# Filler products for TensorE in layer 1 and gate weights in three loads, in a two-layer decode kernel

## The chip, the cores and the metric

The kernel runs on one core of one Trainium2 chip. The metric is the device time of one execution in microseconds (us). Executions of one kernel agree here within about 0.3%, so a change of a few tenths of a microsecond is at the edge of what the times can show.

## The reference, cut to what matters

One token goes through two layers with the same weights. Each layer is an attention over the last 4096 positions of a cache (32 heads of width 192), then a gated feed-forward part (640 to 1536 to 640). Both add to a residual.

```python
x = x + A(layernorm(x), k_cache, v_cache, wq, wo)   # softmax(q k^T) v, 32 heads, window 4096
x = x + B(layernorm(x), w_gate, w_up, w_down)       # down(sigmoid(gate(x)) * up(x))
x = x + A(layernorm(x), ...)                        # the same weights and cache again
x = x + B(layernorm(x), ...)
```

With one token there is almost no reuse. The kernel keeps a part of the cache on the chip for the second layer, but it still reads 218 MB in 0.51 ms.

## The kernel before

Heads go in 16 pairs. The keys of pair p and the values of pair p-1 come in one load of 7.3 MB (128 rows of 56,832 B, 7,104 KB in the views), into alternating buffers. All big loads are issued in order on one queue; each waits until TensorE has finished with the buffer it will overwrite. A step of layer 1 (`l == 0` in the code), cut:

```python
def step(p, prev):
    if l == 0 and prev > 0:
        ev = PVn(prev - 1, 1 - prev % 2)   # output projection of an older pair; frees its value buffer
    Q(p, 0)                                # query, waits for the load of pair p
    QK(p, 0)                               # scores, 24 products of 512 columns
    soft(0, ...)                           # DVE maximum, ACT diag, PE transpose of it, DVE
    expo()                                 # ACT exponential
    PVmm(prev, prev % 2)                   # value products, 32 of 384 columns
    ET(p % 2)
    PVt(prev % 2)
```

After the steps comes the last pair, whose values are in three pieces, and then the feed-forward part. Its weights pass through one region that holds 19 blocks of 640 columns, so the later loads overwrite blocks whose products are done (cut, with `...`):

```python
# key: (cell of the region, first block, end block)
MW = {"wg0": (0, 0, 3), "wg1": (3, 3, 6), "wg2": (6, 6, 9), "wg3": (9, 9, 12), "u0": (12, 0, 2), "u1": (14, 2, 7),
      "d0": (0, 0, 3), "d1": (3, 3, 6), "u2": (6, 7, 10), "u3": (9, 10, 12), "d2": (11, 6, 9), "d3": (14, 9, 11), "d4": (16, 11, 12)}
MD = {"wg0": (0, 0, 6), "wg2": (6, 6, 12), ...}      # the loads: gate weights in two, the rest as in MW
MAFTER = {"d0": ("wg0",), "d1": ("wg1",), "u2": ("wg2",), "u3": ("wg3",), ...}   # d0 is loaded after the products of wg0
...
            PVmm(p, 1)          # end of layer 1, p = 15
            RS(1, 2)
            PVn(p - 1, 0)
            PVt(1, False)
            PVn(p, 1)
        return residual(xi)     # then layer norm, gate, up and down products
```

## Time and profile before

| what | value |
|---|---|
| median of 6 runs (lowest to highest) | 513.63 us (513.21 to 513.99) |
| read from HBM | 218.2 MB, 426 GB/s over the span |
| TensorE busy | 51% of the span, mean granted clock 0.623 |
| chain of waits | 64% DMA, 22% TensorE |

The page of the kernel before: busy times, then the span in 40 slices (granted clock and DMA share in tenths, and GB/s), the chain that ended last, and the group of value products (busy us and mean ns of one, then idle time before them).

```profile
PE 262.5 (51%) x3716; PEld 138.4 (27%) x3716; DVE 101.5 (20%) x385; ACT 85.1 (17%) x171; POOL 4.3 (1%) x31
...
PEclk9955665565566775566575578675655566555855
DMA  9999999999999999999999999999999999999996
GB/s 426 426 427 426 427 430 428 430 453 444 426 430 430 431 435 426 430 448 444 399 420 412 409 440 434 432 430 427 450 439 435 430 430 439 431 431 413 434 424 280
...
DMA 64%; PE 22%; DVE 8%; ACT 3%; issue 2%; SPq 1%; DVEq 0%; POOL 0%; ACTq 0%; POOLq 0%
...
L494 PE MATMUL o<-big,et_sb 128*2 128x384 bf16 x1024 | 77.4, 471 | 8.5 <-DMA big<-in_uc_dram 4.2
```

The DMA row is at its highest step in 39 of 40 slices, and the chain is mostly DMA. The table of windows for the same kernel, with the stretch where layer 1 ends:

```profile
core 0: us, PE busy (x) PEld busy (x) DVE busy (x) ACT busy (x) POOL busy (x), PEclk, DMA share, GB/s
40.00:240.00 200.00, 93.24 (x1233) 45.72 (x1233) 35.77 (x125) 30.24 (x60) 1.07 (x12) 0.60 1.00 432
257.70:288.00 30.30, 18.20 (x342) 12.17 (x338) 5.24 (x29) 4.35 (x10) 0.09 (x1) 0.58 1.00 411
277.00:288.00 11.00, 6.38 (x154) 5.63 (x154) 1.22 (x8) 0.73 (x3) 0.00 (x0) 0.50 1.02 398
```

The last three columns are the ones to read: clock, DMA share, GB/s. (These views count a packet, with its bytes and its time, where it starts. In a window of a few us rates and shares are therefore rough.) In the steps the stream moves 432 GB/s. Around the feed-forward part it moves 411, in its core 398 (share 1.02).

The timeline of TensorE in the kernel before (start, duration, then in brackets the idle time before and what ended it):

```profile
246.85 0.56 PE L414 MATMUL bank<-sh,big 128*128 128x1 bf16 x15 [5.94 <-DMA big<-in_uc_dram]
...
252.27 0.80 PE L448 MATMUL bank<-diag,sc 128*128 128x128 f32 x2 [1.76 <-ACT diag L445]
253.00 2.73 PE L494 MATMUL o<-big,et_sb 128*2 128x384 bf16 x32
...
274.86 0.96 PE L684 MATMUL scores<-sh,big 128*128 128x1 bf16 x30 [0.61 <-DVE bank L670]
277.15 0.96 PE L684 MATMUL scores<-sh,big 128*128 128x1 bf16 x30 [1.34 <-DMA big<-in_wg_dram]
...
279.85 0.83 PE L684 MATMUL scores<-sh,big 128*128 128x1 bf16 x25 [1.05 <-DMA big<-in_wu_dram]
```

The first lines are one step: TensorE waits 5.94 us for the pair load, later 1.76 us for diag, then takes 2.73 us for the value products at half clock. The last three are the gate and up products.

### The profile page before, as it was taken

The numbers are of one execution on the slowest core, as the hardware profiler recorded it, in microseconds if no ns is written. First come the engines' busy times: TensorE is split into PE (matmuls) and PEld (weight loads), VectorE is DVE, ScalarE is ACT, GpSimd is POOL, SyncE is SP. The second block draws the span as 40 slices with busy tenths as digits, with TensorE's granted clock in tenths as the row PEclk, the third lists the DMA queues.
The fourth block names the chain that finished last, engine by engine and source line by source line (L and its number), as shares of the span: only waits on it lengthen the run. The fifth ranks groups of instructions, "written<-read, shape, count | busy, mean of one in ns | idle before, by whom it ended". The sixth has DMA issues, their size and how long they took to land.

```text
span 512.2 us, 8583 instructions
## 1 busy us (share of the span) xinstructions
PE 262.5 (51%) x3716; PEld 138.4 (27%) x3716; DVE 101.5 (20%) x385; ACT 85.1 (17%) x171; POOL 4.3 (1%) x31
## 2 busy tenths in 40 slices
PE   0352455344643254436566767774725344634565
PEld 0221222122311122222234424442312122312234
DVE  0221212112210221112121343231202112210311
ACT  1110111011100111011121024221211011101220
POOL 0010000000000000000000000000000000000000
PEclk9955665565566775566575578675655566555855
DMA  9999999999999999999999999999999999999996
GB/s 426 426 427 426 427 430 428 430 453 444 426 430 430 431 435 426 430 448 444 399 420 412 409 440 434 432 430 427 450 439 435 430 430 439 431 431 413 434 424 280
DMA packets 9676, 218.47 MB, mean 427 GB/s; under 512 B 1208, under 2 KB 1592, under 8 KB 4664
## 3 DMA queue, kind: packets, MB, share of 16 engines
q1 hardware_dynamic: 9512, 218.14, 99.2%
q8 instruction: 13, 0.21, 0.1%
q10 hardware_dynamic: 144, 0.06, 0.0%
q14 instruction: 7, 0.06, 0.0%
HBM read 218.20 MB, written 0.00 MB: 426 GB/s over the span
## 4 chain that ended last, share of the span: by engine, by line
DMA 64%; PE 22%; DVE 8%; ACT 3%; issue 2%; SPq 1%; DVEq 0%; POOL 0%; ACTq 0%; POOLq 0%
DMA big<-in_uc_dram 54%; PE scores L432 8%; DMA big<-in_wd_dram 6%; PE o L494 6%; DMA big<-in_wu_dram 4%; DVE sc L442 3%; PE bank L448 2%; ACT e_sb L458 2%; PE bank L414 2%; PE bank L529 1%; SPq L217 1%; PE bank L464 1%; ACT diag L445 1%; DVE sc L477 1%; DVE qs L420 1%
## 5 line engine op out<-in xcount | busy, mean ns | idle before, releaser
L432 PE MATMUL scores<-big,qs 128*32 128x512 bf16 x744 | 82.0, 608 | 10.3 <-DVE qs L420 9.6
L414 PE MATMUL bank<-sh,big 128*128 128x1 bf16 x465 | 17.0, 166 | 130.9 <-DMA big<-in_uc_dram 128.5
L494 PE MATMUL o<-big,et_sb 128*2 128x384 bf16 x1024 | 77.4, 471 | 8.5 <-DMA big<-in_uc_dram 4.2
L445 ACT ACTIVATE diag<-cst,sc 128x128 f32<-128x128 bf16 x32 | 12.8, 401 | 304.8 <-DVE sc L442 296.8
L442 DVE TENSOR_REDUCE sc<-scores 128x1 f32<-128x1024 f32 x31 | 37.9, 1224 | 77.8 <-PE scores L432 77.8
L414 PEld LDWEIGHTS bank<-sh,big 128*128 128x128 bf16 x465 | 14.6, 103 | 134.0 <-DMA big<-in_uc_dram 112.2
L448 PE MATMUL bank<-diag,sc 128*128 128x128 f32 x64 | 22.5, 447 | 46.7 <-ACT diag L445 46.7
L458 ACT ACTIVATE e_sb<-scores,sc 128x1024 bf16<-128x1024 f32 x31 | 37.4, 1205 | 42.1 <-DVE sc L453 39.9
L494 PEld LDWEIGHTS o<-big,et_sb 128*2 128x2 bf16 x1024 | 28.4, 107 | 44.2 <-issue 29.9
L420 DVE TENSOR_TENSOR qs<-bank,cst 128x96 bf16<-128x96 f32 x30 | 7.7, 258 | 159.6 <-PE bank L414 159.6
L432 PEld LDWEIGHTS scores<-big,qs 128*32 128x32 bf16 x744 | 24.3, 131 | 43.0 <-issue 29.5
L448 PEld LDWEIGHTS bank<-diag,sc 128*128 128x128 f32 x64 | 14.1, 276 | 72.7 <-ACT diag L445 70.4
L501 ACT CAST o_sb<-o 128x384 bf16<-128x384 f32 x64 | 29.7, 474 | 22.7 <-PE o L494 22.4
L529 PE MATMUL bank<-sh,big 128*128 128x1 bf16 x480 | 17.1, 165 | 14.9 <-DVE sh L518 14.9
L468 DVE CAST et_sb<-bank 128x64 bf16<-128x64 f32 x32 | 7.2, 225 | 71.1 <-PE bank L464 71.1
L529 PEld LDWEIGHTS bank<-sh,big 128*128 128x128 bf16 x480 | 14.5, 99 | 17.4 <-DVE sh L518 12.1
L449 DVE TENSOR_REDUCE sc<-bank 128x2 f32<-128x128 f32 x32 | 9.3, 292 | 43.3 <-PE bank L448 43.3
L464 PE MATMUL bank<-cst,e_sb 128*128 128x8 bf16 x256 | 11.7, 169 | 6.8 <-ACT e_sb L458 6.7
L464 PEld LDWEIGHTS bank<-cst,e_sb 128*128 128x128 bf16 x256 | 9.0, 102 | 23.0 <-issue 16.5
L475 PE MATMUL o<-sc 128*128 128x2 f32 x62 | 13.7, 291 | 0.6 <-ACT o_sb L501 0.6
L475 PEld LDWEIGHTS o<-sc 128*128 128x128 f32 x62 | 11.8, 239 | 2.0 <-ACT o_sb L501 1.3
L477 DVE RECIPROCAL sc<-o 64x1 f32<-64x1 f32 x62 | 10.2, 165 | 9.5 <-PE o L475 7.9
(80 smaller groups left out, 109.5 us busy)
## 6 DMA issues: line engine op xcount, KB each, us to landing
big<-in_uc_dram SPq DMA_DIRECT2D x20, 7104.0 KB, 22.6
big<-in_uc_dram SPq DMA_DIRECT2D x11, 3552.0 KB, 20.6
big<-in_uc_dram SPq DMA_DIRECT2D x2, 3072.0 KB, 18.6
big<-in_uc_dram SPq DMA_DIRECT2D x8, 480.0 KB, 7.4
big<-in_uc_dram SPq DMA_DIRECT2D x1, 2784.0 KB, 13.3
big<-in_uc_dram SPq DMA_DIRECT2D x1, 2304.0 KB, 10.7
big<-in_uc_dram SPq DMA_DIRECT2D x1, 2048.0 KB, 12.1
big<-in_wg_dram SPq DMA_DIRECT2D x2, 960.0 KB, 16.2
```

What stands on the lines that cost most here:

```text
L414: ins = t.matmul(qe[:, i:i + 1], lhsT=w[:, c * 2 * DH + c0:c * 2 * DH + c0 + P], rhs=xq[:, c:c + 1], start=(c == 0), stop=(c == DC - 1))
L432: ins = t.matmul(sc_x[1 + b][32 * j:32 * j + 32, :], lhsT=qs[:, y, k, :], rhs=slot(sa, WQE + k * W + (4 * b + j) * 512, 512), start=(k == ...
L442: pg.op("dve", lambda v: v.reduce_max(out=mx, in_=sc_x[0][:], axis=AX.X), wr=[res("mx")], ex=sc_x[3:5])
L445: pg.op("act", lambda a: a.mul(out=diag[:], in_=ident, mul=mx), rd=[res("cst"), res("mx")], wr=[res("diag")])
L448: pg.op("pe", lambda t: t.matmul(dmx[:, 0:P], lhsT=ones_f, rhs=diag[:], start=True, stop=True), rd=[res("diag"), res("ones")], ex=[rb[2]])
L458: pg.op("act", lambda a: a.activation(out=e_sb[:], in_=sc_x[0][:], func=ACT.Exp, bias=nbias, scale=srs_c, accum_out=rowsum), rd=[res("nbia ...
L464: ins = t.matmul(qe[:, 0:2 * NB].rearrange("p (r x) -> p r x", r=2)[:, :, 4 * b:4 * b + 4], lhsT=e_sb[:, b * P:(b + 1) * P], rhs=sel, star ...
L475: pg.op("pe", lambda t: t.matmul(sm, lhsT=ones_f, rhs=rs2[z], start=True, stop=True), rd=[res(f"rs2{z}"), res("ones")], wr=[res("rsum")], ...
L477: rb[bk].last["dve"] = pg.op("dve", lambda v, h=h: v.reciprocal(out=Rn[z][64 * h:64 * h + 64], in_=sm[64 * h:64 * h + 64, h:h + 1]), rd=[r ...
L494: ins = t.matmul(o8[h][32 * j:32 * j + 2, 0:2 * DH].rearrange("p (a d) -> p a d", a=2), lhsT=et_sb[:, z, h * NB + 2 * u:h * NB + 2 * u + 2 ...
L501: pg.op("act", lambda a, h=h: a.copy(out=o8_sb[:, :, h * DH:(h + 1) * DH], in_=o8[h][:, 0:2 * DH].rearrange("p (a d) -> p a d", a=2)), wr= ...
L529: ins = t.matmul(yT[:, j:j + 1], lhsT=wo[:, c * D + j * P:c * D + (j + 1) * P], rhs=oTb[z][:, c:c + 1], start=False, stop=(c == 2), skip_g ...
```

## The change

The intent: if TensorE is kept busier, its granted clock should rise. So products that nobody uses are put into its waits, into PSUM banks (the buffers that its results go to in this kernel) that are idle then. Faster value products should release buffers earlier. And the gate weights come as 3, 6 and 3 blocks in place of 6 and 6, so that the first products, and the loads that wait for them, start earlier.

```diff
-    MD = {"wg0": (0, 0, 6), "wg2": (6, 6, 12), ...}
+    MD = {"wg0": (0, 0, 3), "wg1": (3, 3, 9), "wg3": (9, 9, 12), ...}
+        def spin(n, *bks):
+            for i in range(n):
+                bk = bks[i % len(bks)]
+                m = 2 * DH if bk in (4, 5) else 512
+                pg.op("pe", lambda t, bk=bk, m=m: t.matmul(bank[bk][:, 0:m], lhsT=ident, rhs=slot(...), start=True, stop=True), ...)
-        def PVmm(p, z):
+        def PVmm(p, z, mid=None):
+                    if part == 0 and mid is not None:
+                        mid()                      # ahead of the last piece of the last values
             Q(p, 0)
             QK(p, 0)
+            if l == 0:
+                spin(3, 4, 5)
             soft(0, ...)
-            PVmm(p, 1)
+            spin(4, 0, 1)
+            PVmm(p, 1, lambda: spin(2, 0, 1))
```

More of the change, by code (lines that the diff above doesn't have):

```diff
@@ L186, in decode_kernel @@
           "d0": (0, 0, 3), "d1": (3, 3, 6), "u2": (6, 7, 10), "u3": (9, 10, 12), "d2": (11, 6, 9), "d3": (14, 9, 11), "d4": (16, 11, 12)}
-    MD = {"wg0": (0, 0, 6), "wg2": (6, 6, 12), **{k: v for k, v in MW.items() if k[0] != "w"}}
+    MD = {"wg0": (0, 0, 3), "wg1": (3, 3, 9), "wg3": (9, 9, 12), **{k: v for k, v in MW.items() if k[0] != "w"}}
     MAFTER = {"d0": ("wg0",), "d1": ("wg1",), "u2": ("wg2",), "u3": ("wg3",), "d2": ("wg3", "u0"), "d3": ("u1",), "d4": ("u1",)}
@@ L438, in QK @@
             return ev
+        def spin(n, *bks):
+            for i in range(n):
+                bk = bks[i % len(bks)]
+                m = 2 * DH if bk in (4, 5) else 512
+                pg.op("pe", lambda t, bk=bk, m=m: t.matmul(bank[bk][:, 0:m], lhsT=ident, rhs=slot(A_SLOT[0][0], WQE, m), start=True, stop=True),
+                      rd=[res("cst"), rslot[A_SLOT[0][0]]], ex=[rb[bk]])
         def soft(x=0, hook=None, mid=None, late=None):
```

## The prediction

> **What bounds the kernel now.** The DMA stream. The page puts the DMA share in the highest step in 39 of 40 slices, with 218.2 MB read at 426 GB/s over a span of 512.2 us; the chain of work that ended last is 64% DMA, 22% PE; TensorE is busy 51%. In the table of windows, 40 to 240 us has DMA share 1.00 and 432 GB/s; the stretch that the change aims at, 257.7 to 288 us, also has 1.00, but 411 GB/s. From the trace's packet records I count about 16 packets in flight in every microsecond from 2 to 506 us, so an earlier release has no hole to fill. The lower rate goes with packet size: packets of 56,832 B took 2,099 ns (433 GB/s over 16 engines), of 7,680 B 292 ns (420), of 3,840 B 154 ns (400).
>
> **What the change does.**
> 1. Wide products (three of 384 columns) go between scores and softmax in the 15 steps of the first layer, six of 512 around its last value product. Nothing uses them. They fall into waits that the timeline shows: TensorE idle from 250.5 to 252.3 us (reduction 1.24 us, diag 0.41), 266.9 to 268.5 and 269.6 to 270.3. I estimate 0.32 us for 384 columns at clock 0.50 from the score products (0.43 us between groups of 512); three are about 1 us, inside the 1.8 us wait. Their purpose is a warm clock: the Trainium skill, "TensorE: Matmul & The Clock Gate", section "Part 1: The HAM clock gate (the 'warmup' mystery)", says that some 3.4 us of sustained activity lifts the clock from half. Scores plus filler are 3.8 us, so some value products should shorten from 2.7 us (32 matmuls) towards 1.6. This trace agrees that the clock matters: scores took 2.75 us at 0.50, 1.84 where it was near full.
> 2. Releases then come perhaps 0.5 to 1 us earlier. But a pair load is issued 10.8 us after the last landing, while the one in flight takes 16.6 us (7.1 MB at 433 GB/s): 6 us of slack. The burst issued from 257.7 us is queued 5 to 19 us ahead of landing. Worth nothing in time.
> 3. Gate weights as 3, 6, 3 blocks: the first products wait for the layer norm (274.86 us, released by DVE) anyway; the middle six start about 1.1 us earlier than 277.15, the last three land as before. Up and down weights still bound the rest (each group waits for DMA). Cost: 128 packets of 7,680 B become 256 of 3,840 B: 128 x (2 x 154 - 292) / 16 = 0.13 us on a saturated stream, and one more issue of 0.43 us on a queue far ahead.
>
> **Share on the critical path.** Fillers none; of the split, the 0.13 us.
>
> **Predicted time:** 513.8 us, 8 in 10 between 513.0 and 514.6. Chances: faster by over 2% 0.01, within 2% 0.98, slower by over 2% 0.01.
>
> **What would show it.** Right: mean clock above 0.62, busy time of value products (77.4 us) down by 5 to 20 us, waits for pair loads up by as much, DMA share and GB/s of the slices kept, and 33.4 us per two pair landings kept. Wrong: GB/s of 257 to 290 us above 420, or pair landings coming earlier.
>
> **What would make it wrong.** Fillers ending so late that releases overrun the 6 us of slack; the longer loop body fetching instructions again during the loop (16 KB packets of 0.9 us each); a shifted fetch hitting the last loads, at most 0.9 us; the chip's scatter of a few tenths.

## More of the kernel before

The view of the issuing queue has the first two loads of down weights; they wait for the first gate products:

```profile
275.45 0.80 SPq L217 DMA_DIRECT2D big<-in_wd_dram  x2
```

## The result, and the profile after

| kernel | median of 6 runs (lowest to highest) |
|---|---|
| before | 513.63 us (513.21 to 513.99) |
| after | 513.72 us (513.59 to 514.20) |

The ratio is 1.0003, with a 95% interval of 0.999 to 1.0016: no difference is resolved. (Here and below a ratio is the mean time of one kernel's runs over that of the other's of the same rounds, so not quite the ratio of the medians.)

The page of the changed kernel, with the lines that answer to those of before. Line numbers moved: L494 is L503 now, and L444 is the filler.

```profile
PE 265.9 (52%) x3766; PEld 137.2 (27%) x3767; DVE 101.7 (20%) x385; ACT 84.2 (16%) x171; POOL 4.2 (1%) x31
...
PEclk9996777677756655557686588765857555556655
DMA  9999999999999999999999999999999999999996
GB/s 417 439 423 426 423 432 427 435 444 435 444 426 435 427 435 426 430 444 448 398 422 415 410 436 441 429 427 430 453 448 430 430 426 430 427 436 419 432 424 280
...
DMA 68%; PE 19%; DVE 7%; ACT 2%; issue 2%; SPq 1%; DVEq 0%; POOL 0%; ACTq 0%; POOLq 0%
...
L503 PE MATMUL o<-big,et_sb 128*2 128x384 bf16 x1024 | 68.1, 426 | 8.1 <-DMA big<-in_uc_dram 3.3
...
L444 PE MATMUL o<-big,cst 128*128 128x384 bf16 x45 | 15.4, 474 | 0.0
```

The clock row is higher in most slices of layer 1, and the value products fell from 77.4 to 68.1 us. The 45 fillers of the steps cost 15.4 us of busy time. DMA share is the same in every slice, and so is the mean of GB/s. The table of windows:

```profile
40.00:240.00 200.00, 99.25 (x1272) 47.23 (x1272) 36.20 (x126) 29.83 (x60) 1.06 (x12) 0.64 1.00 432
257.70:288.00 30.30, 20.40 (x338) 12.29 (x339) 5.08 (x28) 4.14 (x10) 0.09 (x1) 0.68 1.00 413
277.00:288.00 11.00, 6.00 (x140) 5.25 (x139) 1.13 (x7) 0.73 (x3) 0.00 (x0) 0.50 1.02 406
```

The steps (40 to 240 us) kept 432 GB/s at a clock of 0.64 in place of 0.60. The timeline of TensorE after the change, two steps and the end of the layer:

```profile
217.33 1.14 PE L444 MATMUL o<-big,cst 128*128 128x384 bf16 x3
...
219.90 2.73 PE L503 MATMUL o<-big,et_sb 128*2 128x384 bf16 x32
...
250.85 0.85 PE L444 MATMUL o<-big,cst 128*128 128x384 bf16 x3
...
253.10 1.47 PE L503 MATMUL o<-big,et_sb 128*2 128x384 bf16 x32
...
271.41 0.65 PE L503 MATMUL o<-big,et_sb 128*2 128x384 bf16 x8
...
275.13 0.54 PE L696 MATMUL scores<-sh,big 128*128 128x1 bf16 x15 [0.35 <-DVE sc L374]
276.06 0.96 PE L696 MATMUL scores<-sh,big 128*128 128x1 bf16 x30 [0.39 <-DMA big<-in_wg_dram]
277.22 0.56 PE L696 MATMUL scores<-sh,big 128*128 128x1 bf16 x15 [0.20 <-DMA big<-in_wg_dram]
```

Both steps have the three fillers. After the one at 217.33 the value products are still cold (2.73 us), after the one at 250.85 they are warm (1.47). Of 15 steps, 10 had warm value products in this trace and 3 in that of before. The last piece of the last values started at 271.41 us, against 270.28 before: at this place the fillers delayed TensorE.

The clock records kept with the traces say when the clock was granted. In the kernel before it was full for 3.4 or 6.8 us in 12 of the 15 steps as well, but in nine of these too late for the value products: in the step around 50 us these ran from 52.0 to 54.7 us at a clock of 0.50, and the clock was full from 54.5 to 57.9. After the change it was full from 49.9 to 56.7 us, and the value products took 1.47 us from 52.1 on. In each of the fourteen traces all changes of the clock lie on one grid of 3.41 us. Five such intervals are 17.1 us and a step is 16.7 us, so the grid shifts by 0.3 us from step to step. That fits warm steps coming in runs of several.

The first loads of down weights, which the split was to bring forward, were issued 0.25 us later than before (275.45):

```profile
275.70 1.28 SPq L217 DMA_DIRECT2D big<-in_wd_dram  x2
```

The time that the faster products saved became waiting. The list of waits, kernel before and then after (us in total, times, longest):

```profile
PE bank L414 <- DMA big<-in_uc_dram: 128.5, 21, 11.8
```

```profile
PE bank L414 <- DMA big<-in_uc_dram: 136.5, 22, 12.0
```

Waiting for the pair loads rose by 8.0 us, about the 9.3 us by which value products became shorter. In the kernel before the next pair load was issued about 10 us after the landing before it in a step with warm value products, and about 11 us after it in a cold one; so it was after the change. The change made more steps warm, and the pairs still landed every 16.7 us.

### The profile page after: what moved, and what is told of

It is laid out like the page before. It is cut to its first block, busy times and chain, and to the rows that moved or that the text cites. A ratio compares the mean times of both kernels' runs of the same rounds, so it can differ in the third digit from the quotient of the medians.

```text
span 512.2 us, 8685 instructions
## 1 busy us (share of the span) xinstructions
PE 265.9 (52%) x3766; PEld 137.2 (27%) x3767; DVE 101.7 (20%) x385; ACT 84.2 (16%) x171; POOL 4.2 (1%) x31
## 4 chain that ended last, share of the span: by engine, by line
DMA 68%; PE 19%; DVE 7%; ACT 2%; issue 2%; SPq 1%; DVEq 0%; POOL 0%; ACTq 0%; POOLq 0%
DMA big<-in_uc_dram 58%; PE scores L432 7%; DMA big<-in_wd_dram 6%; PE o L503 5%; DMA big<-in_wu_dram 4%; DVE sc L449 3%; PE bank L455 2%; PE bank L414 2%; PE bank L538 1%; ACT e_sb L465 1%; SPq L217 1%; ACT diag L452 1%; PE bank L471 1%; DVE sc L484 1%; DVE qs L420 1%
## 5 line engine op out<-in xcount | busy, mean ns | idle before, releaser
L414 PE MATMUL bank<-sh,big 128*128 128x1 bf16 x465 | 17.1, 166 | 138.4 <-DMA big<-in_uc_dram 136.5
L503 PE MATMUL o<-big,et_sb 128*2 128x384 bf16 x1024 | 68.1, 426 | 8.1 <-DMA big<-in_uc_dram 3.3
L503 PEld LDWEIGHTS o<-big,et_sb 128*2 128x2 bf16 x1024 | 26.2, 100 | 39.1 <-issue 20.5
L455 PE MATMUL bank<-diag,sc 128*128 128x128 f32 x64 | 19.9, 403 | 32.3 <-ACT diag L452 32.3
L455 PEld LDWEIGHTS bank<-diag,sc 128*128 128x128 f32 x64 | 12.4, 241 | 53.2 <-ACT diag L452 51.6
L471 PE MATMUL bank<-cst,e_sb 128*128 128x8 bf16 x256 | 11.6, 169 | 11.1 <-ACT e_sb L465 11.0
L444 PE MATMUL o<-big,cst 128*128 128x384 bf16 x45 | 15.4, 474 | 0.0
L484 DVE RECIPROCAL sc<-o 64x1 f32<-64x1 f32 x62 | 10.2, 165 | 9.0 <-PE o L482 7.5
(84 smaller groups left out, 124.0 us busy)
## 6 DMA issues: line engine op xcount, KB each, us to landing
big<-in_uc_dram SPq DMA_DIRECT2D x1, 2048.0 KB, 11.4
```

What stands on the lines that cost most here:

```text
L414: ins = t.matmul(qe[:, i:i + 1], lhsT=w[:, c * 2 * DH + c0:c * 2 * DH + c0 + P], rhs=xq[:, c:c + 1], start=(c == 0), stop=(c == DC - 1))
L444: pg.op("pe", lambda t, bk=bk, m=m: t.matmul(bank[bk][:, 0:m], lhsT=ident, rhs=slot(A_SLOT[0][0], WQE, m), start=True, stop=True), rd=[res ...
L455: pg.op("pe", lambda t: t.matmul(dmx[:, 0:P], lhsT=ones_f, rhs=diag[:], start=True, stop=True), rd=[res("diag"), res("ones")], ex=[rb[2]])
L471: ins = t.matmul(qe[:, 0:2 * NB].rearrange("p (r x) -> p r x", r=2)[:, :, 4 * b:4 * b + 4], lhsT=e_sb[:, b * P:(b + 1) * P], rhs=sel, star ...
L484: rb[bk].last["dve"] = pg.op("dve", lambda v, h=h: v.reciprocal(out=Rn[z][64 * h:64 * h + 64], in_=sm[64 * h:64 * h + 64, h:h + 1]), rd=[r ...
L503: ins = t.matmul(o8[h][32 * j:32 * j + 2, 0:2 * DH].rearrange("p (a d) -> p a d", a=2), lhsT=et_sb[:, z, h * NB + 2 * u:h * NB + 2 * u + 2 ...
```

## The experiments

Four theories were tried against each other:

- **A**: the DMA stream is the bound and has reserve; TensorE's time does not matter until about 6 us of slack per step are used up.
- **B**: the chain through TensorE bounds, and the fillers' own time eats what they save.
- **C**: the fillers gain and the finer gate loads lose as much.
- **D**: the end of layer 1, where the end fillers and the new split act, is bound by TensorE.

### The two halves of the change alone

Fillers only, gate weights as before:

```diff
-    MD = {"wg0": (0, 0, 3), "wg1": (3, 3, 9), "wg3": (9, 9, 12), ...}
+    MD = {"wg0": (0, 0, 6), "wg2": (6, 6, 12), ...}
```

> Only the fillers, gate weights in two loads of six as before. Theory A (the DMA stream is the bound, TensorE has about 6 us of slack per step): same as before, 513.6 within 0.3 us. Rival C (fillers gain, the split of the gate weights costs as much, and the two cancel): faster than before by 0.3 us or more. Rival B (the chain through TensorE bounds, and the fillers' 17 us of busy time eat the 9 us that they save): no clear difference either; B is told apart by the runs with more fillers.

Measured: 513.58 us (5 runs), ratio 0.9997 (0.9983 to 1.001).

The split only, no fillers:

```diff
-    MD = {"wg0": (0, 0, 6), "wg2": (6, 6, 12), ...}        # in the kernel before
+    MD = {"wg0": (0, 0, 3), "wg1": (3, 3, 9), "wg3": (9, 9, 12), ...}
```

> Only the gate weights in 3, 6, 3 blocks, no fillers. Theory A: before plus about 0.1 us (estimate from packet times of before: 128 x (2 x 154 - 292) / 16 = 0.13 us), so 513.6 to 513.9, not resolved. Rival C: slower than before by 0.3 us or more.

Measured: 513.55 us (5 runs), ratio 0.9996 (0.9982 to 1.001). Neither half moves the time by an amount that is resolved, so theory C has nothing to stand on. The intervals reach to 0.9 us either way, so two effects of 0.3 us that cancel are unlikely by the medians but not excluded. The trace of this run also had warm value products in 6 of 15 steps, without any filler. The clock scatters from run to run: the seven full-size kernels without fillers in the steps had 72.3 to 77.4 us of value products (mean 75.1), the three with three fillers per step 67.8 to 69.0 (mean 68.3). So the fillers are worth about 7 us of TensorE's time, not the 9.3 that one pair of traces shows.

### Many more fillers: how much slack a step has

```diff
-                spin(3, 4, 5)
+                spin(36, 4, 5)      # second run: spin(80, 4, 5)
```

> 36 fillers of 384 columns in each of the 15 steps in place of 3 (estimate 0.32 us each cold, 0.16 warm: about 6.3 us, some 4.5 us more than the wait hides). Theory A: no change, 513.7 within 0.5 us, the wait for pair loads falls from about 6 us to 2 or 3 us per step. Rival B: each of 15 steps is 3 us or more longer, together 45 us or more: about 560 us.

Measured: 533.58 us (4 runs), ratio 1.0376 (1.0355 to 1.0397). Theory A's "no change" is wrong, and so is B's 560. The timeline of this kernel shows a step with its release and the next landing:

```profile
121.93 7.16 PE L444 MATMUL o<-big,cst 128*128 128x384 bf16 x36
...
133.37 0.33 SPq L217 DMA_DIRECT2D big<-in_uc_dram  x1
135.30 0.48 PEld L414 LDWEIGHTS bank<-sh,big 128*128 128x128 bf16 x15 [2.09 <-DMA big<-in_uc_dram]
```

The next pair load was issued at 133.37 us, 1.93 us before the load in flight landed at 135.30. By A's sum that is early enough. The table of windows around it shows that it was not:

```profile
132.00:134.00 2.00, 0.84 (x21) 0.67 (x21) 0.57 (x4) 0.00 (x0) 0.00 (x0) 1.00 0.20 85
134.00:136.00 2.00, 0.56 (x15) 0.48 (x15) 0.10 (x1) 0.00 (x0) 0.09 (x1) 0.63 1.26 426
```

Packets that started from 132 to 134 us carried only 85 GB/s. (With each packet's bytes spread over its duration, the stream moved 231 GB/s in the first of these windows and 239 in the second, in place of 433.) The packet records say why. The 16 DMA engines do not finish together: the first ran out of work at 132.6 us, 2.7 us before the landing was seen by TensorE, and the first packet of the new load started at 134.34, 1.0 us after its issue. At this landing a load would have had to be issued about 3.7 us ahead. The spread varies: in the five gaps of this run that cost most, the first engine ran out 1.5 to 3.6 us before the landing. Between 46 and 263 us, loads issued 2.7 us or less before the next landing made the following pair land 2.0 to 3.3 us late (five of twelve), and loads issued 3.3 us or more before it only 0.2 to 0.6 us (seven). In the kernel before, a load issued at 140.71 us was followed by the landing at 146.33, 5.6 us later. The slack of such a cold step was therefore about 2 to 3 us, not 6. The releases came at 13.9 to 16.4 us after a landing in place of 10.0 to 11.6, some 4 us later, and that is over the slack.

> 80 fillers per step, an estimated 13.5 us. Theory A: TensorE's step is then about 21 us, longer than the 16.7 us between pair landings, so the slack is used up and the time grows by about 4 us in each of some 14 steps: about 570 us, 550 to 590. If the time still did not change, A's figure of 6 us of slack would be wrong.

Measured: 593.91 us (4 runs), ratio 1.1547 (1.1522 to 1.1573). A step now lasts about 21 us and in the steps that I read TensorE does not wait for a pair load, as expected; the time is a little above the range. With 36 fillers the stream ran dry in some steps and not in others; with 80 it did so in every step that I read. No run lies between 3 and 36 fillers, so where the loss begins is an estimate from the packet records, not a measured edge.

### A finer split than the change's

```diff
-    MD = {"wg0": (0, 0, 6), "wg2": (6, 6, 12), ...}
+    MD = {**{f"wg{i}": (i, i, i + 1) for i in range(12)}, ...}
```

> The split made larger: gate weights in twelve loads of one block, no fillers. Packets: 256 of 7,680 B (292 ns) become 1,536 of 1,280 B (56 ns): (1536 x 56 - 256 x 292) / 16 = 0.7 us more on the stream. Theory A: before plus about 0.7 us (0.4 to 1.0). If the cost of packets were not on the bound: no change.

Measured: 514.88 us (5 runs: two near 513.9, three near 515.0), ratio 1.0018 (1.0005 to 1.0032), which is 0.3 to 1.6 us. The estimate of 0.7 us from packet times lies inside. In the trace, of one of the two faster runs, the last up weights of the burst landed 11.9 us after the first of the last values in place of 11.4, and they had been issued 8.7 us before, so it was not a late issue. So small packets cost something on this stream, in the range of what their durations add up to; for the change's own split the same sum gives 0.13 us, which no run here resolves.

### Delays at the end of layer 1

```diff
             PVn(p, 1)              # kernel before, last output product of layer 1
+            spin(10, 4, 5)         # second run: spin(40, 4, 5)
```

> Before, with ten products of 384 columns after the last output product of layer 1: a delay of TensorE by an estimated 2 to 3 us just where the change aimed, ahead of the layer norm and the gate products. Theory A: the loads of the down weights are issued 4 us ahead of the end of the queue, so little or nothing: 513.6 to 514.2 us. If the end of layer 1 were bound by TensorE (rival D: the split and the end fillers act on the bound there), the time would grow by the whole delay, 2 to 3 us.

Measured: 515.96 us (4 runs), ratio 1.0043 (1.0028 to 1.0059). The first loads of down weights were issued at 277.95 us in place of 275.45:

```profile
277.95 0.81 SPq L217 DMA_DIRECT2D big<-in_wd_dram  x2
```

A delay of 2.5 us cost 2.3 us. Theory A expected 0.6 at most; here D's number is the right one. The window from 277 to 288 us, for which before had 398 GB/s:

```profile
277.00:288.00 11.00, 5.51 (x168) 4.99 (x167) 1.39 (x10) 0.73 (x3) 0.00 (x0) 0.66 0.95 343
```

> Before, with forty such products at the same place: a delay of an estimated 7 to 8 us. Theory A: the queue runs dry after about 3 to 4 us of delay, so the time grows by about 4 us (2.5 to 6), not by the whole 7 to 8; a hole of low DMA share appears around 280 to 285 us. Rival D: plus 7 to 8 us.

Measured: 518.68 us (4 runs: two near 517.2, two near 520.4), ratio 1.0087 (1.0062 to 1.0112). The median lost 5.0 us, inside theory A's range of 2.5 to 6. But the runs fall in two groups, 3.5 and 6.7 us above the kernel before, and only the slowest was traced; how long the fillers delayed the other runs is not known. In the traced run the issue came at 283.24 us, 7.8 us later than before, and the time was 7.0 us longer, about the whole delay:

```profile
283.24 0.80 SPq L217 DMA_DIRECT2D big<-in_wd_dram  x2
```

The DMA view from 276 to 288 us, in slices of 0.3 us (share in tenths, GB/s):

```profile
DMA  9999999543420000000000000009496798999999
GB/s 431 478 422 384 401 499 414 235 192 128 140 85 0 0 0 0 0 0 0 0 0 0 0 0 0 0 0 166 90 192 179 294 384 358 422 422 435 384 384 410
```

The stream dries up from 278 us over about 1.5 us, as one engine after another runs out, and stands still until 284.2, 1.0 us after the issue. The slack at this place is the delay less the loss: 7.8 - 7.0 = 0.8 us in this run and 2.5 - 2.1 = 0.4 us in the traced run of the smaller delay (515.74 us), each uncertain by the few tenths by which times scatter. The prediction had called this queue "far ahead".

### No waits at all there

If a delay costs nearly its whole length, would an advance gain? This kernel puts the down weights and the second part of the up weights into another buffer, over keys that layer 2 needs, so its result is wrong. All their loads are then issued in the first burst, with no wait for products.

```diff
-    MAFTER = {"d0": ("wg0",), "d1": ("wg1",), "u2": ("wg2",), ...}
+    MAFTER = {}
+    XO = {"d0": 0, "d1": 3, "u2": 6, "u3": 9, "d2": 11, "d3": 14, "d4": 16}
-            pg.dma(q_dma(mreg(c * FW, ...), ...), k, wr=rc[c:c + f1 - f0])
+            if k in XO:
+                pg.dma(q_dma(slot(4, XO[k] * FW, ...), ...), k, wr=[res("x" + k)], extra=list(rslot[4].rd))
             ...
```

> Before, with the waits at the end of layer 1 taken away: the down weights and the second part of the up weights of the first feed-forward part go into another buffer (over the keys of head pair 0, wrong result on purpose), so that all their loads are issued in the one burst from about 258 us, with no wait for the gate and up products. Same bytes, same packets. This is the most that an earlier release there can be worth. Revised theory A2 (the stream is the bound, and at the end of layer 1 the loads are issued only just in time, so that packets between 277 and 287 us stretch by about 0.4 us in all): 0.2 to 0.6 us faster than before, and no stretched packets in that stretch. First theory A (the queue is far ahead): no change. Rival D (the end of layer 1 is bound by TensorE): 1 us faster or more.

Measured: 513.68 us (5 runs) against 514.05 for before on the same chip, ratio 0.9993 (0.9979 to 1.0007). The window from 277 to 288 us:

```profile
277.00:288.00 11.00, 5.80 (x152) 5.13 (x152) 1.02 (x6) 0.74 (x3) 0.00 (x0) 0.50 1.02 414
```

The stream went from 398 to 414 GB/s there (400 to 415 with each packet's bytes spread over its duration). Over 11 us, that is 16 / 414 x 11 = 0.4 us, and the medians differ by 0.37 us, but the times alone do not resolve it. The traced run, at 514.41 us, was the slowest of its five, and from the landing of the first of the last values to its end it took no less time than the kernel before (242.2 us against 242.1): the lead at the end of layer 1 was gone later, and no run shows where it went. So about 0.4 us is an estimate of the most that an earlier release at the end of layer 1 can be worth, not a measured gain. D's "1 us or more" lies at the edge of the interval (up to 1.1 us faster) and is unlikely on the gaining side.

Why did 398 GB/s go with a share of 1.02? In the packet records of before, some packets between 277 and 287 us are stretched: a few of 3,840 B, which as a rule take 149 ns, took 300 to 1,500. Their excess over the usual duration, summed and divided by 16 engines, is 0.38 us in before, 0.18 after the change, 0.07 with the split only, 0.03 here and 1.10 with the small delay. An engine with a stretched packet counts as busy and moves little. The cause of a single stretched packet is not seen in the trace. The extremes go with how late the loads are issued; in between the order does not hold (the kernel before issued earlier than the changed one and has twice its sum).

### The opposite of the split: fewer, larger loads

```diff
-    MD = {..., "u0": 2 blocks, "u1": 5, "d0": 3, "d1": 3, "u2": 3, "u3": 2, "d2": 3, "d3": 2, "d4": 1}
+    MD = {..., "u0": (12, 0, 7), "d0": (0, 0, 6), "u2": (6, 7, 12), "d2": (11, 6, 12)}
-    MAFTER = {"d0": ("wg0",), "d1": ("wg1",), ...}
+    MAFTER = {"d0": ("wg1",), "u2": ("wg2", "wg3"), "d2": ("wg3", "u0", "u1")}
-    MV = {..., "v0": (6, 9), "v2": (9, 11), "v3": (11, 14), "v4": (14, 17)}
+    MV = {..., "v0": (6, 11), "v3": (11, 17)}
```

> The opposite of the split, to see whether a version beats both: up, down and refilled value loads of layer 1's feed-forward part joined to fewer, larger ones (up 2+2 loads to 1+1, down 5 to 2, refill 5 to 3), no fillers. Estimate from packet times (154 ns for 3,840 B, 104 for 2,560 B, 56 for 1,280 B, 244 for 6,400 B, 292 for 7,680 B, about 340 for 8,960 B): about 0.7 us less on the stream. Theory A: before minus 0.7 us if the queue does not run dry, so 512.9; if later releases let the queue run dry (each joined load waits for the later of its parts), nothing or slower.

Measured: 515.92 us (5 runs), ratio 1.0039 (1.0026 to 1.0053): slower by 2 us where the packet sum promised 0.7 us less. The window from 277 to 288 us:

```profile
277.00:288.00 11.00, 4.31 (x124) 3.99 (x125) 0.85 (x4) 0.73 (x3) 0.00 (x0) 0.50 1.00 365
```

The share is 1.00 and the rate 365 GB/s. Packets of 6,400 B took 293 ns on average in place of 244, of 7,680 B 316 in place of 292. The joined loads wait for the later of their parts: they were issued at 275.75, 278.05 and 280.84 us, and in the kernel before the first parts went out at 275.45, 277.74 and 278.83. The stretched packets add up to 1.2 us from 277 to 287 us and 1.1 us after it. Which of the joins costs most was not separated.

The Trainium skill, "Perfetto Trace Analysis", section "DMA Optimizations", recommends larger transfers on a saturated stream as the primary optimization. For packet cost alone the finer split above agrees with it. But where loads wait for buffers, the same section's second point, that splitting may let some parts start sooner, fits what was measured here, although the page sees the gain where engines are generally idle: the small loads issued early beat the large ones issued late.

### With the stream out of the way

Eleven pair loads are cut to 40% of their bytes, so TensorE's chain bounds these steps; the rest of the buffer keeps old data and the result is wrong. One run is on the kernel before, one on the changed kernel.

```diff
-            pg.dma(q_dma(slot(first, 0, 2 * UNIT), uc[p]), ...)
+            nl = 11360 if l == 0 and p > 3 else 2 * UNIT
+            pg.dma(q_dma(slot(first, 0, nl), uc[p][:, 0:nl]), ...)
```

> Wrong result on purpose: before, with eleven pair loads of the first layer cut to 40% of their bytes (stale data in the rest), so that a load takes about 6.7 us and TensorE's chain (about 10.5 us) bounds those steps. Theory A: the time falls by about 11 x (16.7 - 10.5) = 68 us, to about 445 us (430 to 460). If bytes did not bound: no change.

Measured: 441.78 us (4 runs), ratio 0.8598 (0.8583 to 0.8614). The steps took about 10.2 us; 11 x (16.7 - 10.2) = 71.5 us, and 71.9 were saved. So the bytes of the stream are the bound of these steps, directly shown.

> The same cut loads, with the whole change. Here TensorE's chain bounds the eleven steps, so what the fillers save there must show: theory A expects 0 to 1.2 us less per step (value products 2.7 us cold, 1.5 warm) than the cut kernel without fillers, 0 to 13 us together; nothing if the shorter waits keep the clock warm without fillers. Rival B: slower than the cut kernel without fillers.

Measured: 441.92 us (4 runs), the same. The fillers gain nothing here, where TensorE's chain bounds. The timeline of one such step:

```profile
159.12 1.14 PE L445 MATMUL o<-big,cst 128*128 128x384 bf16 x3
...
161.67 2.73 PE L504 MATMUL o<-big,et_sb 128*2 128x384 bf16 x32
```

The fillers ran and the value products stayed at 2.73 us; in both cut kernels the value products of all eleven cut steps were cold. What a step gains where TensorE bounds and the clock is warm was therefore not tested. Steps of 10.2 us are close to three of the 3.4 us windows that the skill describes ("TensorE: Matmul & The Clock Gate", "Part 1: The HAM clock gate (the 'warmup' mystery)"), so each step may meet the window at the same phase. The clock records agree: in this trace the clock was full for 3.4 us from 83.0, 103.5, 124.0, 144.4 and 164.9 us, in every second step, each time just after value products had ended (at 82.6 us in the first case); in the cut kernel without fillers, too, it was full only as they ended or later. Why the steps settled at this phase is not shown. The page says that the window is free-running; that three fillers warm some steps and not others, and 36 warmed all 14 that I read from the trace, agrees with it.

### The change without the end fillers

```diff
-            spin(4, 0, 1)
-            PVmm(p, 1, lambda: spin(2, 0, 1))
+            PVmm(p, 1)
```

> The change without the six fillers of 512 columns around the last value product. Same time as before (within 0.3 us) by every theory here. For the layer norm at the end of layer 1, which came 0.5 us later with the change than before: if the end fillers delay it, the last output product of layer 1 ends earlier here than with them (about 273.2 us against 274.1), otherwise as late.

Measured: 513.34 us (4 runs), ratio 0.9991 (0.9973 to 1.0009). It is the lowest median of the kernels with all their bytes, but not resolved from before. The first gate products:

```profile
274.30 0.51 PE L695 MATMUL scores<-sh,big 128*128 128x1 bf16 x15 [0.35 <-DVE sc L374]
```

They started at 274.30 us, against 275.13 with the end fillers and 274.86 before. In the trace of the changed kernel the end fillers worked against their purpose: the fillers ahead of the last values ended at 266.8 us and the values came at 268.4, so the products of the first pieces ran cold (2.09 us), and the second pair of fillers then stood in front of the last piece. In the trace of the kernel with the fillers only, the same end fillers did what they were meant to do:

```profile
269.22 1.15 PE L503 MATMUL o<-big,et_sb 128*2 128x384 bf16 x24 [0.56 <-DMA big<-in_uc_dram]
270.30 0.61 PE L444 MATMUL scores<-big,cst 128*128 128x512 bf16 x2
271.05 0.50 PE L503 MATMUL o<-big,et_sb 128*2 128x384 bf16 x8
```

From the landing of the last piece to the first product of the layer norm it took 4.2 us in the changed kernel, 3.1 us with the fillers only, and 3.4 to 3.5 us in the three traces without end fillers (before, split only, this one). So the sign of the end fillers' effect is open, and the 0.8 us is one run's number. No version beats both kernels beyond noise.

## Why the prediction was right or wrong

- **The total** was right: 513.8 us foretold, 513.72 measured, no gain and no loss over noise. The bound was named rightly: the cut loads saved what their bytes predict, and TensorE's savings went into waits for loads.
- **Step 1, the fillers**, was right in kind. The clock rose to 0.672 in the traced run and value products fell by 9.3 us, of which about 7 are the fillers' and the rest scatter between traces. What it left out is that the clock was raised in most steps before as well, mostly too late for the value products. A single trace of each kernel is a weak test of a clock effect: before's own runs had mean clocks from 0.545 to 0.675.
- **Step 2, "6 us of slack", was mis-sized**: in the warm steps the releases did come about 0.9 us earlier, and it was worth nothing, but the slack of a cold step is about 2 to 3 us. The sum "time of a load less time to the issue" left out that engines run out of work before the landing is seen, 2.7 us in the gap shown, and that the first packet starts 1.0 us after the issue. The 36 fillers cost 20 us where the prediction's sum gave none.
- **"So an earlier release has no hole to fill" failed** in its smaller part. Counting packets in flight finds no hole, but stretched packets hide one of about 0.4 us at the end of layer 1. The kernel with no waits there recovers it in GB/s; that it gains time was not shown.
- **"A queue far ahead" failed for the loads after the burst.** It held for the burst issued from 257.7 us. The loads of down weights, which wait for the gate products, are issued with 0.4 to 0.8 us to spare. In the changed kernel the first of them went out 0.25 us later than before, which is inside that. That it cost nothing is luck: the prediction did not know how little there was to spare.
- **Step 3, the split**: the middle six blocks started at 276.06 us, 1.1 us earlier than before, and the last three at 277.22, as foretold. The first three started at 275.13, 0.3 us later than the first six before, though their load had landed at 273.72 us in place of 274.81. That the first products waited for the layer norm was a misreading. The matmul line named a DVE release, but its DVE work (a memset) was the last thing to end among several; with the split the same products start right after the layer norm, at 274.56 us in the run with the split only and 274.30 without end fillers. In before they had waited for the load of six blocks. The cost of 0.13 us is not resolved; the larger split supports the way it was worked out.

## What to carry to other kernels

Where DMA is the bound, as here, look for what time saved on another engine can still fill: here it turned into waiting, and the only dip was in GB/s, not in DMA share. Slack has two sides: measure it by adding a known delay, because a queue that looks some microseconds ahead may have almost none, as here, once the spread of the DMA engines and the start of a load are taken off. Before joining loads to save packet cost, ask which release each part waits for.

## What the Trainium skill lacked or had wrong

- "DMA: Bandwidth & Descriptors", "Why a DMA increments its semaphore by 16 and not by 1", says that the engines finish independently, and not by how much. Here the first engine ran out 2.7 us before TensorE saw the landing of a 7.3 MB load (1.5 to 3.6 us in the five costliest gaps of that run), and the drain at the end of layer 1 took about 1.5 us. That spread used up about half of the 5.6 us by which a load was ahead.
- "Perfetto Trace Analysis", "DMA Engine Tracks", says that the slices of an engine show busy time without idle time. In the merged kernel the DMA share was 1.00 at 365 GB/s, and packets of 6,400 B took 293 ns on average in place of 244. Its advice in "Identifying the Most-Contended Engine", to read bandwidth in place of occupancy for DMA, is the one that held.
- "TensorE: Matmul & The Clock Gate" does not say how reliably a short filler warms the clock. Three fillers after 2.75 us of scores left 10, 8 and 10 of 15 steps warm (value products under 2 us) in three traces, against 3 to 7 without them in seven; in the cut kernels none of the eleven cut steps, with or without them.
